# Two chunks' decay steps out of the first order, a block's plan turned by two units, and some low parts by TensorE, in a fused recurrence and feed-forward kernel

## The chip, the cores and the metric

One core of a Trainium2 chip. The metric is the device time of one execution in microseconds; of the kernel before three runs are shown, with a median of 519.06 us (518.17 to 519.08).

## The reference

A linear recurrence over 768 steps for 4 sequences and 8 heads of 48 channels, and a two-layer feed-forward with the gate h cos(h) on its output, for 3072 rows:

```python
for t in range(S):
    cur = einsum('bhd,bhe->bhde', u * k[t], v[t])
    y[t] = einsum('bhd,bhde->bhe', r[t], state + cur)
    state = w[t][..., None] * state + einsum('bhd,bhe->bhde', k[t], v[t])
...
h = x @ w_in                 # 3072 x 384 by 384 x 2048
out = (h * cos(h)) @ w_out   # 2048 x 384
```

## The kernel before

**Work.** The sequences are cut into 24 chunks of 128 steps (numbers 0 to 23 in the order in which they are taken); two chunks make a block of 256 rows, so there are 12 blocks. For each chunk the recurrence is put into products over the chunk, with running products of the decays; for each block the feed-forward runs over 8 units of 256 hidden channels. Every product of the feed-forward is taken with operands split into a high and a low part (fp32r), three products for one: high by high, high by low, low by high. The 16 weight blocks are loaded in a packed form in the first stage, turned to high and low parts, and stay.

**Names in the orders.** A number behind a name is a chunk, a block, a unit or a weight block; `+n` in a plan counts from the block at work. For a chunk: ld/load its r, k and decays, lv/v its values, lr its r and k by rows; e the backward scan of decays (line 254), f a reciprocal and the forward scan (259, 260), W a copy of the whole products; k and r the products of k and r with them (269, 271, 273); q and pc, cd (chunks under 6) or m, u, c (later ones) the diagonal; A the diagonal put into a tile by GpSimd (306); a the scores on TensorE (345, 353), P their masked copy by VectorE (363, 366); t and K a transpose and its copy; d, pp the state's decay. For a block: o, p the outputs of the recurrence (429 to 448), s the new states (397), n their sum; xh and xl (X) the high and low part of x. For a unit: mm1 (line 519, in the first order m0.t and m1.t, its two halves), the gate's steps I (ScalarE, 483), S (VectorE, 486), N (ScalarE's sine, 499), M (VectorE, 500), H (high part, ScalarE), L (low part, GpSimd, line 168), and mm2 (538). For a weight block: raw the load, wl and wg two unpackings by ScalarE (185, 189), wy their sum by VectorE (197), wc the high part by ScalarE (193), wx the low part by VectorE (199). Helpers at lines 165 and 168 hold all copies and subtractions.

**Order.** Each engine works through its own instructions in order, and the order is written by hand. `START` is the first order, one list for all five engines: everything of blocks 0 and 1 and of the weights, with the first decay steps of later chunks among it. Its units run in the sequence that `PAIR` gives (a 0 is block 0, a 1 is block 1). `Dn` issues n fillers (line 649): products of the identity by itself, in fp32, two instructions each, into a bank that the next mm1 overwrites. From block 2 on the eight rows of `PLAN` say what goes with each unit of a block; mm2 follows mm1 by two units. `FIRST` replaces the first rows for block 2 (six rows before), `LAST` those at the end. In the last units the decays are also checked (`check_decays`, from `slots - CHECK` on).

**Buffers that the argument touches.** mm1 writes one of two banks ("h" in `BANKS`, in the steady blocks), which the M of two units earlier frees. `maskf` is made by GpSimd, and its 8-bit copy `mask` by VectorE at line 707, ahead of `START`.

Of the kernel before, what the change touches and what calls it, by code (L numbers as in the profile page):

```python
# [70 lines left out]
m0.4 I3 wg8 q5 M2 e5 pc5 wc6 H2 L1 S3 m1.4 m0.5 v4 I4 wy9 N3 S4 cd4 mm2.1 wx6 wg7 wc9 M3 m1.5 wx9 N4 H3 L2 M4 wl7 I5  # L71
wl8 wy7 mm2.2 L3 m0.6 mm2.3 S5 wy8 wc7 wx7 H4 m1.6 raw13 N5 M5 wl11 raw10 e4 wg11 m0.7 wy11 L4 I6 mm2.4 raw12 wc8 S6
wx8 ld6 N6 M6 k5 W4 m1.7 H5 m0.8 k4 cd5 t5 t4 wc11 L5 I7 S7 H6 m1.8 L6 A4 d5 wg10 mm2.5 N7 K4 d4 A5 wl10 W5 I8 raw14
wx11 K5 pp5 M7 m0.9 mm2.6 wy10 S8 H7 N8 wc10 m1.9 f5 M8 wx10 wl12 f4 wl13 I9 m0.10 H8 wg13 S9 L7 N9 r4 mm2.7 a4 L8 e7
m1.10 M9 wg12 wy13 H9 L9 m0.11 wy12 I10 wc13 mm2.8 S10 wg14 m1.11 wx13 P4 raw15 wc12 N10 wx12 I11 M10 wl14 S11 H10 r5
N11 mm2.9 m0.12 s2 M11 wl15 wy14 n2 m1.12 wg15 H11 wy15 m0.13 a5 I12 L10 S12 L11 P5 wc14 wx14 m1.13 wc15 N12 mm2.10 I13
e6 M12 H12 mm2.11 m0.14 S13 wx15 o2 pp4 f6 N13 m1.14 M13 r6 H13 k7 W6 I14 L12 L13 m0.15 S14 p2 N14 xh2.0 k6 m1.15 xl2.0
I15 M14 S15 xh2.1 xl2.1 N15 mm2.12 M15 mm2.13 H14 H15 L14 L15
# [824 lines left out]
```

## Time and profile before

| | us |
|---|---|
| median of three runs (lowest, highest) | 519.06 (518.17, 519.08) |
| the profiled execution, its own time | 517.84 |
| its span, first to last instruction | 516.0 |
| TensorE busy | 508.4 |
| VectorE busy | 390.2 |
| ScalarE busy | 260.2 |
| GpSimd busy | 209.8 |

The span is what the profile shows of one execution; its own time has 1.84 us more around it. A busy time is the union of an engine's instructions, whether they are of use or not. PE stands for TensorE, DVE for VectorE, ACT for ScalarE, POOL for GpSimd, SP for SyncE, which issues the transfers; PEld are TensorE's weight loads, which run beside its products.

### The profile page before, as it was taken

To read this page: it belongs to the slowest core of one execution; us is meant where nothing else is said; L and a number is where in the kernel's file an instruction comes from. 1 tells how busy PE (TensorE), PEld (TensorE's weight loads), DVE (VectorE), ACT (ScalarE), POOL (GpSimd) and SP (SyncE) were. 2 spreads that over 40 slices of the span, in tenths; PEclk is the share of its full clock that TensorE was granted. 3 is DMA by queue.
4 is the path that set the end of the run, shared out by engine and by line. 5 is a ranking of instruction groups with operands and counts; after the bars stand their busy time and mean duration, and the time that the engine had idled before them with its cause. 6 is when DMAs were issued, how large, how long until landed. Compare 5 with 4: busy or idle time off the path is not lost.

```text
span 516.0 us, 12941 instructions
## 1 busy us (share of the span) xinstructions
PE 508.4 (99%) x5432; PEld 494.0 (96%) x5432; DVE 390.2 (76%) x662; ACT 260.2 (50%) x442; POOL 209.8 (41%) x275
## 2 busy tenths in 40 slices
PE   7999999999999999999999999999999999999997
PEld 7999999999999999999999999999999999999996
DVE  8897999977888768758858857947956957678333
ACT  1577997755444444444444444444344454444543
POOL 3361487344435334344334334343533533423330
PEclk9999999999999999999999999999999999999999
DMA  8998083063240151061061060160150130050001
GB/s 246 373 300 268 13 317 109 6 173 120 81 126 32 41 166 32 32 174 32 33 174 33 32 176 6 57 163 15 62 159 25 62 124 1 32 184 1 32 0 36
DMA packets 16733, 52.24 MB, mean 101 GB/s; under 512 B 2016, under 2 KB 8416, under 8 KB 16672
## 3 DMA queue, kind: packets, MB, share of 16 engines
q1 hardware_dynamic: 16528, 51.28, 32.3%
q8 instruction: 44, 0.72, 0.6%
q14 instruction: 17, 0.14, 0.1%
q10 hardware_dynamic: 144, 0.10, 0.1%
HBM read 46.65 MB, written 4.72 MB: 100 GB/s over the span
## 4 chain that ended last, share of the span: by engine, by line
PE 91%; DVE 4%; ACT 2%; DMA 1%; issue 1%; SPq 0%
PE ph L519 38%; PE acc L538 36%; PE filled L649 3%; PE pa L353 3%; PE py L429 2%; PE pst L397 2%; PE py L434 2%; PE pt L375 1%; PE pa L345 1%; PE py L448 1%; DVE h L197 1%; DMA u_by_head<-ut 1%; PE py L444 1%; DVE w L199 1%; PE pc L282 1%
## 5 line engine op out<-in xcount | busy, mean ns | idle before, releaser
L168 POOL TENSOR_TENSOR gs<-rr,gs 128x256 fp32r<-128x256 f32 x188 | 153.8, 838 | 240.7 <-ACT gs L165 235.9
L519 PE MATMUL ph<-xT,w 128*128 128x256 f32 x1728 | 222.4, 282 | 0.3
L519 PEld LDWEIGHTS ph<-xT,w 128*128 128x128 f32 x1728 | 213.0, 188 | 3.2 <-issue 0.6
L538 PE MATMUL acc<-w,gs 128*128 128x384 f32 x1152 | 215.2, 337 | 0.0
L538 PEld LDWEIGHTS acc<-w,gs 128*128 128x128 f32 x1152 | 196.1, 188 | 0.0
L499 ACT ACTIVATE rr<-rr,quarter 128x512 f32<-128x512 f32 x96 | 69.5, 724 | 96.6 <-DVE rr L486 96.5
L486 DVE SCALAR_TENSOR_TENSOR rr<-rr,ph 128x512 f32<-128x512 int32 x96 | 65.5, 682 | 69.4 <-ACT rr L483 68.9
L165 ACT CAST gs<-rr 128x512 fp32r<-128x512 f32 x96 | 59.5, 620 | 68.7 <-DVE rr L500 47.9
L500 DVE TENSOR_TENSOR rr<-rr,ph 128x512 f32<-128x512 f32 x96 | 65.5, 682 | 24.8 <-ACT rr L499 22.3
L483 ACT ACTIVATE rr<-ph 128x512 int32<-128x512 f32 x96 | 57.3, 597 | 48.9 <-PE ph L519 48.3
L306 POOL TENSOR_SCALAR_AFFINE_SELECT asb<-cd 128x512 f32<-128x512 f32 x48 | 41.6, 891 | 42.2 <-DVE cd L296 27.2
L366 DVE COPY_PREDICATED asb<-turned_mask,pa 64x128 f32<-64x128 uint8 (+1 forms) x108 | 33.6, 346 | 1.7
L260 DVE TENSOR_TENSOR_SCAN tt<-tt,inj 112x516 f32<-112x516 f32 x24 | 32.0, 1334 | 0.8
L254 DVE TENSOR_TENSOR_SCAN ee<-tt,one_e 112x516 f32<-112x516 f32 x24 | 31.9, 1328 | 0.1
L649 PE MATMUL filled<-ident 128*128 128x128 f32 x180 | 23.5, 289 | 1.9 <-POOL ident masks.py:199 1.9
L649 PEld LDWEIGHTS filled<-ident 128*128 128x128 f32 x180 | 22.3, 203 | 2.1 <-POOL ident masks.py:199 1.9
L185 ACT ACTIVATE h<-raw 128x768 int32<-128x768 uint32 x16 | 14.6, 916 | 13.0 <-DMA raw<-wts 11.9
L168 DVE TENSOR_TENSOR xT<-py,xT 128x384 fp32r<-128x384 f32 x24 | 12.3, 550 | 11.2 <-ACT xT L165 11.2
L165 ACT COPY past<-dd 48x192 f32<-48x192 f32 x40 | 14.0, 351 | 11.3 <-DVE dd L329 11.0
L197 DVE CUSTOM_DVE_ANT_0 h<-h,top 128x1536 uint16<-128x1536 uint16 x16 | 17.0, 1071 | 3.2 <-ACT cd L165 1.8
L189 ACT ACTIVATE top<-raw 128x768 f16<-128x768 bf16 x16 | 17.3, 1079 | 0.0
L199 DVE TENSOR_TENSOR w<-h,w 128x768 fp32r<-128x768 f32 x16 | 15.6, 973 | 0.3 <-ACT w L193 0.3
(77 smaller groups left out, 363.2 us busy)
## 6 DMA issues: line engine op xcount, KB each, us to landing
tt<-tr SPq DMA_DIRECT2D x22, 674.2 KB, 7.3
raw<-wts SPq DMA_DIRECT2D x16, 767.8 KB, 9.4
rk<-tn SPq DMA_DIRECT2D x18, 384.0 KB, 3.0
v<-tv SPq DMA_DIRECT2D x24, 224.0 KB, 5.5
ww<-w SPq DMA_DIRECT2D x6, 768.0 KB, 5.6
out<-ob SPq DMA_DIRECT2D x23, 192.0 KB, 2.0
tt<-tr SPq DMA_DIRECT2D x4, 224.0 KB, 4.6
tt<-tr SPq DMA_DIRECT2D x2, 226.2 KB, 3.8
```

Of the source, the lines that this page charges most:

```text
L165: (nc.scalar.copy if E[name] is nc.scalar else E[name].tensor_copy)(out=out, in_=in_)
L168: E[name].tensor_tensor(out=out, in0=full, in1=high.bitcast(F32), op=ALU.subtract)
L260: nc.vector.tensor_tensor_scan(out=wp[:, 0:W129], data0=wp[:, 0:W129], data1=inj.rearrange("p a t -> p (a t)"), initial=0.0, op0=ALU.mult, ...
L306: nc.gpsimd.affine_select(out=asb, in_=col.unsqueeze(2).to_broadcast([C, NP, C]), pattern=[[0, 4], [1, C]], compare_op=ALU.is_equal, fill= ...
L366: nc.vector.copy_predicated(*(which(x) for x in (a["asb", h], turned_mask, pa[h])))
L483: nc.scalar.activation(made["rr"].bitcast(I32), ph, AF.Copy, scale=INV2PI / W_SCALE, bias=0.25)
L486: nc.vector.scalar_tensor_tensor(out=made["rr"], in0=made["rr"].bitcast(I32), scalar=-2.0 * math.pi * W_SCALE, in1=ph, op0=ALU.mult, op1=A ...
L499: N=lambda: nc.scalar.activation(made["rr"], made["rr"], AF.Sin, scale=1.0 / W_SCALE, bias=quarter),
L500: M=lambda: nc.vector.tensor_tensor(out=made["rr"], in0=made["rr"], in1=ph, op=ALU.mult), H=high, L=low)
L519: nc.tensor.matmul(out=ph[:, fi], lhsT=wgt[u * FU + fi][:, 0, a, kt * 128:(kt + 1) * 128], rhs=xT[:, b, kt], start=n == 0, stop=n == 3 * K ...
L538: nc.tensor.matmul(out=accs[i][j][:, :DM], lhsT=gs[:, a, fi, j * C:(j + 1) * C], rhs=wgt[u * FU + fi][:, 1, b], start=u == 0 and fi == 0 a ...
L649: nc.tensor.matmul(out=filled, lhsT=ident, rhs=ident, start=True, stop=True)
```

## The change

- In `START`, e6, f6, W6, r6, k6, e7 and k7 are gone and the order is new; there are 33 fillers where there were 90. W0 becomes `Wa0`, the same copy by ScalarE.
- Weight blocks 0 and 2: wx is replaced by `wp` and `wv`. wp lets TensorE form identity times the whole value (fp32) plus minus-identity times the high part (fp32r) in a bank, for each of two halves; wv copies both to the low part by ScalarE. The same for x of block 0: `xp` adds minus-identity times the high part onto the bank that holds x, and `xa` copies it, in place of xl.
- The negative identity is new, made by ScalarE; it shares its place with `u_sb`, which is taken only when it is loaded.
- `mask` is copied by ScalarE.
- `PLAN`: the former rows 6 and 7 stand first, for the following block, with d of the odd chunk moved to row 3 and u, c, lr in row 1. `FIRST` has eight rows and takes the decay steps of chunks 6 and 7.
- The check of the decays begins 12 units before the end, not 14. `START` and the rest lie in one hand-written schedule, SyncE's part of it for `START` alone.

```diff
-PLAN = ["t+2 t+3 load+6 mm1 K+2 K+3 e+4 I S k+4 N M mm2 H L f+4",
-        "mm1 I S r+4 N M mm2 H L",
+PLAN = ["mm1 I S k+3 N M mm2 H L f+3",
+        "mm1 I S r+3 N M mm2 H L u+3 c+3 lr+5",
+        "t+2 t+3 load+6 mm1 K+2 K+3 e+4 I S k+4 N M mm2 H L f+4",
+        "mm1 I S r+4 N M mm2 H L d+3",
         "a+2 a+3 mm1 P+2 P+3 I S m+4 N M mm2 H L",
         "mm1 I S u+4 N M mm2 H L",
         "o+1 p+1 s+1 mm1 load+7 lv+6 lv+7 X+1 n+1 I S c+4 N M mm2 H L d+4",
-        "mm1 I S m+5 N M mm2 H L e+5 lr+6",
-        "mm1 I S k+5 N M mm2 H L f+5 d+5",
-        "mm1 I S r+5 N M mm2 H L u+5 c+5 lr+7"]
+        "mm1 I S m+5 N M mm2 H L e+5 lr+6"]
 START = """
-ld1 ld0 e1 f1 ld3 q1 raw1 e0 wl1 q0 k1 f0 D18 pc1 W0 q3 W1 r1 r0 wg1 ld2 D24 a1 k0 cd1 wy1 D2 t0 raw0 A1 v0 e2 pc0 P1
-q2 D7 a0 cd0 raw3 wl0 v1 t1 e3 wg0 raw2 K1 K0 raw4 raw5 wc1 wy0 A0 P0 wx1 raw6 wc0 D16 o0 wg2 ld7 k2 xh0.0 f2 pc2 wx0
-xh0.1 xl0.0 wg3 wl2 pc3 xl0.1 v3 cd2 t2 cd3 raw7 k3 wy2 D8 m0.0 f3 wc2 wl3 s0 wx2 wg4 K2 t3 m1.0 r2 wl4 v2 r3 I0 wy3 n0
-wy4 v5 A3 S0 wc3 K3 wg6 W2 A2 ld4 D3 m0.1 wc4 a2 raw9 D7 s1 a3 wx3 N0 wg5 m1.1 P2 n1 I1 P3 M0 H0 wx4 W3 wl5 wy5 D5 o1
-wl6 ld5 wc5 S1 wx5 xh1.0 xl1.0 xh1.1 L0 xl1.1 m0.2 wg9 mm2.0 N1 raw8 q4 M1 m1.2 m0.3 I2 pc4 wl9 S2 wy6 m1.3 raw11 H1 N2
...
+ld1 ld0 e1 raw0 f1 q1 e0 W1 Wa0 wl0 q0 D19 pc1 cd1 wg0 k1 k0 v0 raw1 ld3 A1 f0 r1 v1 D8 t0 pc0 t1 r0 wy0 a1 raw2 K0 K1
+ld2 cd0 wc0 wl1 P1 a0 raw3 wp0 A0 P0 wg1 raw4 v5 o0 e3 wv0 q3 wy1 f3 xh0.0 s0 xh0.1 pc3 wl2 k3 W3 q2 xp0.0 wg2 xp0.1 D3
+pc2 v3 wc1 xa0.0 wy2 e2 xa0.1 wc2 n0 wx1 cd3 cd2 r3 f2 W2 t3 m0.0 wg3 wp2 wl3 wy3 a3 raw5 m1.0 K3 v2 ld4 r2 wv2 A3 A2
+wc3 wl4 raw7 k2 I0 wg4 m0.1 wg5 wx3 P3 t2 a2 m1.1 raw6 wl5 raw8 P2 K2 v4 ld5 raw9 D3 o1 wy4 wy5 wc4 wc5 wx4 S0 s1 m0.2
+xh1.0 wx5 xl1.0 xh1.1 xl1.1 N0 I1 wg6 m1.2 M0 H0 m0.3 q4 I2 S1 L0 N1 S2 wl6 pc4 M1 m1.3 N2 I3 wy6 H1 S3 wc6 m0.4 N3 M2
...
+m0.9 t5 m1.9 k4 wx10 L6 A5 I9 N8 L7 r4 wl12 wx11 S9 wg12 K5 mm2.6 M8 mm2.7 a4 H8 N9 m0.10 wy12 A4 P4 M9 wl13 wg13 L8
+wc12 t4 wy13 m1.10 m0.11 H9 I10 pp5 mm2.8 S10 m1.11 N10 wc13 wg14 wx12 M10 I11 wx13 m0.12 L9 mm2.9 H10 wl14 f5 wg15 S11
...
 """
-FIRST = ["lr+2 lr+3 load+4 load+5 lv+4 lv+5 t+2 t+3 mm1 K+2 K+3 f+3 I S m+2 N M mm2 H L u+2 c+2 lr+4",
-         "mm1 I S r+3 N M mm2 H L m+3 u+3 c+3",
-         "mm1 I S N M mm2 H L d+2 d+3 lr+5 load+6 e+4",
...
+FIRST = ["lr+2 lr+3 load+4 load+5 lv+4 lv+5 mm1 e+2 e+3 k+2 k+3 I S f+2 N M mm2 H L r+2",
+         "mm1 I S f+3 N M mm2 H L r+3",
+         "mm1 t+2 t+3 I S K+2 K+3 N M mm2 H L m+2 u+2 c+2 d+2",
+         "mm1 I S m+3 u+3 N M mm2 H L c+3 d+3 lr+4",
+         "a+2 a+3 mm1 P+2 P+3 I S e+4 N M mm2 H L k+4",
+         "mm1 I S f+4 N M mm2 H L r+4 load+6",
+         "o+1 p+1 s+1 mm1 load+7 lv+6 lv+7 X+1 n+1 I S N M mm2 H L m+4 u+4 c+4 d+4",
+         "mm1 I S m+5 N M mm2 H L e+5 lr+6"]
-CHECK = 14
+CHECK = 12
@@
+    nident = cst.tile([C, KT, C], F32R, tag="u_sb", name="nident")[:, 0]
+    nc.scalar.activation(nident, ident, AF.Copy, scale=-1.0)
@@
+        def left_over():
+            made["left"] = [bank("a", [128, 512], "left")[:, :DM] for k in range(2)]
+            for k in range(2):
+                nc.tensor.matmul(out=made["left"][k], lhsT=ident, rhs=made["h"][:, k].bitcast(F32), start=True, stop=False, skip_group_check=True)
+                nc.tensor.matmul(out=made["left"][k], lhsT=nident, rhs=wgt[f][:, k, 0], start=False, stop=True, skip_group_check=True)
+
+        def taken():
+            for k in range(2):
+                nc.scalar.copy(out=wgt[f][:, k, 1], in_=made["left"][k])
+
+        part(("wp", f), left_over)
+        part(("wv", f), taken)
@@
+        def less(side):
+            nc.tensor.matmul(out=py[side].rearrange("p k t -> p (k t)"), lhsT=nident, rhs=halves_of["x"][:, 0, side], start=False, stop=True, skip_group_check=True)
+
+        def taken(side):
+            nc.scalar.copy(out=halves_of["x"][:, 1, side], in_=py[side].rearrange("p k t -> p (k t)"))
@@
-    with tc.manual_schedule(engines={ET.PE, ET.DVE, ET.Activation, ET.Pool, ET.SP}):
-        nc.vector.tensor_copy(out=mask, in_=maskf)
-        for token in START.split():
-            at_first(token)
-    engines(LATER)
     up1 = [NU * BLK, NU * BLK - LAG]
     with tc.manual_schedule(engines={ET.PE, ET.DVE, ET.Activation, ET.Pool}):
+        with tc.manual_schedule(engines={ET.SP}):
+            nc.scalar.copy(out=mask, in_=maskf)
+            for token in START.split():
+                at_first(token)
+        engines(LATER)
```

## Rows read from the trace of the kernel before

**Rows 1.** The page's parts 1 and 2: busy time of TensorE; slices.

```profile
PE 508.4 (99%) x5432; PEld 494.0 (96%) x5432; DVE 390.2 (76%) x662; ACT 260.2 (50%) x442; POOL 209.8 (41%) x275
...
PE   7999999999999999999999999999999999999997
...
DVE  8897999977888768758858857947956957678333
...
PEclk9999999999999999999999999999999999999999
```

**Rows 2.** The page's part 5: groups of instructions (busy, mean ns, idle before).

```profile
L486 DVE SCALAR_TENSOR_TENSOR rr<-rr,ph 128x512 f32<-128x512 int32 x96 | 65.5, 682 | 69.4 <-ACT rr L483 68.9
...
L260 DVE TENSOR_TENSOR_SCAN tt<-tt,inj 112x516 f32<-112x516 f32 x24 | 32.0, 1334 | 0.8
L254 DVE TENSOR_TENSOR_SCAN ee<-tt,one_e 112x516 f32<-112x516 f32 x24 | 31.9, 1328 | 0.1
L649 PE MATMUL filled<-ident 128*128 128x128 f32 x180 | 23.5, 289 | 1.9 <-POOL ident masks.py:199 1.9
...
L168 DVE TENSOR_TENSOR xT<-py,xT 128x384 fp32r<-128x384 f32 x24 | 12.3, 550 | 11.2 <-ACT xT L165 11.2
...
L197 DVE CUSTOM_DVE_ANT_0 h<-h,top 128x1536 uint16<-128x1536 uint16 x16 | 17.0, 1071 | 3.2 <-ACT cd L165 1.8
...
L199 DVE TENSOR_TENSOR w<-h,w 128x768 fp32r<-128x768 f32 x16 | 15.6, 973 | 0.3 <-ACT w L193 0.3
```

**Rows 3.** Windows: length; PE, PEld, DVE, ACT, POOL busy; clock; DMA share, GB/s.

```profile
0.00:46.44 46.44, 43.15 (x520) 40.81 (x520) 39.61 (x54) 24.12 (x39) 18.34 (x26) 1.00 0.96 299
46.44:86.06 39.62, 38.83 (x293) 38.16 (x289) 38.35 (x47) 34.70 (x55) 23.34 (x25) 1.00 0.51 178
86.06:116.48 30.42, 30.42 (x334) 28.97 (x332) 26.11 (x40) 18.98 (x30) 13.10 (x14) 1.00 0.30 80
```

**Rows 4.** TensorE's timeline, 0 to 150 us (start, length, instructions, wait before).

```profile
1.87 5.75 PE L649 MATMUL filled<-ident 128*128 128x128 f32 x36 [1.87 <-POOL ident masks.py:199]
8.74 1.02 PE L282 MATMUL pc<-u_by_head,rkt 112*128 112x2 f32 x8 [1.12 <-DMA u_by_head<-ut]
9.63 5.60 PE L649 MATMUL filled<-ident 128*128 128x128 f32 x48
...
46.44 1.33 PE L519 MATMUL ph<-xT,w 128*128 128x256 f32 x9
47.61 2.24 PE L538 MATMUL acc<-w,gs 128*128 128x384 f32 x12
...
84.97 1.16 PE L345 MATMUL pa<-tt 48*128 48x128 f32 x16 [0.54 <-DVE tt L269]
```

**Rows 5.** VectorE's timeline, 0 to 145 us.

```profile
2.44 2.32 DVE L707 CAST mask<-maskf 128x512 uint8<-128x512 f32 x1 [0.37 <-POOL maskf L125]
4.68 1.21 DVE L254 TENSOR_TENSOR_SCAN ee<-tt,one_e 112x516 f32<-112x516 f32 x1
```

**Rows 6.** SyncE's timeline, 0 to 3.6 us: the first loads' issues.

```profile
0.83 2.75 SPq L225 DMA_DIRECT2D tt<-tr  x6
```

**Rows 7.** Transfers issued from 0.5 to 1.0 us: size, us to landing.

```profile
tt<-tr SPq DMA_DIRECT2D x1, 226.2 KB, 2.8
```

**Rows 8.** Groups by line of the whole run, those not on the page.

```profile
L165 ACT CAST xT<-py 128x384 fp32r<-128x384 f32 x24 | 10.5, 482 | 4.5 <-PE py L448 2.7 <-PE py L429 1.5 <-PE py L434 0.2
...
L271 DVE TENSOR_TENSOR tt<-tt,ee 112x256 f32<-112x256 f32 x18 | 10.0, 553 | 0.0
...
L363 DVE COPY_PREDICATED asb<-mask,pa 128x512 f32<-128x512 uint8 x12 | 8.1, 727 | 3.2 <-PE pa L345 3.2
...
L259 DVE RECIPROCAL inj<-ee 112x4 f32<-112x4 f32 x24 | 4.1, 172 | 0.0
```

**Rows 9.** Windows of block 2 and block 3, columns as in rows 3.

```profile
116.50:156.60 40.10, 40.10 (x457) 39.08 (x456) 32.65 (x62) 19.08 (x36) 18.70 (x25) 1.00 0.36 103
156.60:196.80 40.20, 40.20 (x458) 39.12 (x457) 29.98 (x56) 18.52 (x34) 16.24 (x23) 1.00 0.27 77
```

More of the change, by code (lines that the diff above doesn't have):

```diff
@@ L70 @@
-wl6 ld5 wc5 S1 wx5 xh1.0 xl1.0 xh1.1 L0 xl1.1 m0.2 wg9 mm2.0 N1 raw8 q4 M1 m1.2 m0.3 I2 pc4 wl9 S2 wy6 m1.3 raw11 H1 N2
[L71 to L78, printed above, removed]
-"""
-FIRST = ["lr+2 lr+3 load+4 load+5 lv+4 lv+5 t+2 t+3 mm1 K+2 K+3 f+3 I S m+2 N M mm2 H L u+2 c+2 lr+4",
[5 rows of a table removed]
+ld1 ld0 e1 raw0 f1 q1 e0 W1 Wa0 wl0 q0 D19 pc1 cd1 wg0 k1 k0 v0 raw1 ld3 A1 f0 r1 v1 D8 t0 pc0 t1 r0 wy0 a1 raw2 K0 K1
@@ new lines @@
+m1.6 M4 H4 d4 wy8 raw12 M5 raw11 raw10 wl9 I6 wg9 mm2.3 S6 m0.7 L4 N6 wc8 wy9 wc9 pc5 m1.7 mm2.4 cd5 wg10 f4 k5 H5 W4
+I7 M6 n1 wx8 H6 wl10 d5 m0.8 wx9 S7 L5 N7 wg11 wl11 M7 wy10 wy11 mm2.5 raw14 raw13 raw15 m1.8 I8 S8 wc10 wc11 ld7 H7
+m0.9 t5 m1.9 k4 wx10 L6 A5 I9 N8 L7 r4 wl12 wx11 S9 wg12 K5 mm2.6 M8 mm2.7 a4 H8 N9 m0.10 wy12 A4 P4 M9 wl13 wg13 L8
+wc12 t4 wy13 m1.10 m0.11 H9 I10 pp5 mm2.8 S10 m1.11 N10 wc13 wg14 wx12 M10 I11 wx13 m0.12 L9 mm2.9 H10 wl14 f5 wg15 S11
+m1.12 N11 L10 wl15 r5 I12 mm2.10 M11 wy14 m0.13 wc14 K4 S12 a5 wy15 W5 N12 wx14 H11 wc15 M12 m1.13 m0.14 P5 wx15 I13
@@ L86 @@
+H12 L11 S13 mm2.11 N13 pp4 m1.14 I14 M13 H13 m0.15 o2 m1.15 S14 I15 S15 L13 L12 N14 N15 p2 mm2.12 M14 xh2.0 xl2.0 M15
+mm2.13 H15 L15 xh2.1 s2 H14 xl2.1 ld6 n2 L14
+"""
+FIRST = ["lr+2 lr+3 load+4 load+5 lv+4 lv+5 mm1 e+2 e+3 k+2 k+3 I S f+2 N M mm2 H L r+2",
[7 rows of a table added]
 LAST = "mm1 I S N M", "mm1 I S N M mm2 h l", "mm2 h l"
-CHECK = 14
+CHECK = 12
 PAIR = "0001110101010101"
@@ L134, in rwkv_cos_ffn @@
     halves = cst.tile([R96, 2], F32, name="halves")
-    u_sb = cst.tile([C, DM], F32, name="u_sb")
     u_by_head = cst.tile([R, NP, 2], F32, name="u_by_head")
@@ L230, in att_load @@
         if j == BY_PE:
-            E["qt"].dma_start(out=u_sb, in_=u.to_broadcast([C, DM]))
+            told["u"] = cst.tile([C, DM], F32, tag="u_sb", name="u_sb")
+            E["qt"].dma_start(out=told["u"], in_=u.to_broadcast([C, DM]))
     def att_load_rk(a):
@@ L291, in att_diag @@
             part(("m", a["j"]), lambda: E["rk"].tensor_tensor(out=rk, in0=rk, in1=a["rk"][:, 1], op=ALU.mult))
-            part(("u", a["j"]), lambda: E["ru"].tensor_tensor(out=rk, in0=rk, in1=u_sb, op=ALU.mult))
+            part(("u", a["j"]), lambda: E["ru"].tensor_tensor(out=rk, in0=rk, in1=told["u"], op=ALU.mult))
             def sums():
@@ L464, in att_past @@
             part(("xl", (i, side)), lambda side=side: low(side))
+            if i <= BLK:
+                part(("xp", (i, side)), lambda side=side: less(side))
+                part(("xa", (i, side)), lambda side=side: taken(side))
     def att_x(a):
@@ L637, in at_first @@
     def at_first(token):
+        by = re.match(r"(W|H|wc)([av])(\d+)$", token)
+        if by:
+            name = dict(W="whole", H="gh", wc="whi0")[by[1]]
+            usual, E[name] = E[name], dict(a=nc.scalar, v=nc.vector)[by[2]]
+            parts.pop((by[1], int(by[3])))()
+            E[name] = usual
+            return
+        if token[:2] == "wp":
+            parts.pop(("wx", int(token[2:])))
+        if token[:2] == "wx":
+            for x in "wp", "wv":
+                parts.pop((x, int(token[2:])))
+        if token[:2] == "xp":
+            parts.pop(("xl", (int(token[2]), int(token[4]))))
+        if token[:2] == "xl":
+            for x in "xp", "xa":
+                parts.pop((x, (int(token[2]), int(token[4]))))
         n, at, side = re.match(r"(mm2\.|m[01]\.|[a-zA-Z]+)(\d+)(?:\.(\d))?$", token).groups()
```

1 line of the change is left out of this document (added), and 3 rows, old and new, of the table FIRST.

## The prediction

> **What bounds the kernel now.** I read the page's busy times first: TensorE is busy 508.4 of 516.0 us, and in the 40 slices it shows a gap in the first alone, while VectorE stands at 9 tenths in a run of slices near the start [rows 1]. So outside its first stage the kernel can become shorter only by doing less on TensorE. Among the groups of instructions one is no work at all: 180 instructions of line 649, the fillers, which multiply the identity by itself and whose result nobody reads [rows 2]. All 90 of them stand in the first order. By the windows, that stage ends at 116.48 us; in its first part, up to the first half of block 0's third unit (m0.2, at 46.44), TensorE is busy 43.15 us although all the fillers lie there, and VectorE 39.61; from there to 86.06 TensorE has 38.83 of 39.62, VectorE 38.35, ScalarE 34.70; after that both have room [rows 3]. The start is thus bound by the inputs of TensorE's work, with fillers in the waits; the middle is full on three engines; the rest is TensorE alone. A wait that shows this is in TensorE's timeline: at 84.97 the scores of chunk 4 stood 0.54 us for VectorE's product on line 269 [rows 4].
>
> **What the change does, part by part.** *Fillers.* The first order before has D18 24 2 7 16 8 3 7 5, which is 90; the new one D19 8 3 3, which is 33. Those taken out lie in the stretch that ran at 48 instructions in 5.60 us, two to a filler, so 0.233 us each [rows 4]. 57 x 0.233 = 13.3 us off TensorE's queue.
>
> *Low parts by TensorE.* wp0 and wp2 replace two subtractions of VectorE. Each is two products of 384 columns in full fp32 and two in fp32r. No fp32 product of 384 columns is in the trace. From above: at the fillers' pace per column it is 3 x 0.233 = 0.70 us; the fp32r one is 0.19 (12 of line 538 in 2.24, [rows 4]); so 2 x (0.70 + 0.19) = 1.78 each, 3.6 for both. From below: if all ran at line 538's pace, 4 x 0.19 x 2 = 1.5. I take the upper end, since the filler is the same form of product. The two xp add 2 x 0.19 = 0.4. Together 4.0, from below 1.9. Each adds a wait: wp0 for ScalarE's wc0, with o0 queued behind it, wp2 for wc2, with a3 and m1.0 behind. o0 waits for P0 in any case, which VectorE's list has behind wy0, the source of wc0; and wx1, for m1.0, stands behind wy2. So both are covered, as long as ScalarE keeps up.
>
> TensorE's sum to the end of the stage is then -13.3 + 4.0 = -9.3 us, all else being the same instructions: the two lists hold the same products. That holds if the inputs come as much earlier. At m0.2 it asks for 46.44 - 9.3 = 37.1 us.
>
> *VectorE ahead of m0.2.* I compared the two lists' VectorE entries before m0.2: 45 before, 35 after, and none that is new. Gone from there are the low parts of weights 0, 2 and 5 (3 x 0.97), four of x (4 x 0.55), one S and one M (2 x 0.68), and n1, which is ScalarE's [rows 2]. The mask's copy, 2.32 us, goes to ScalarE [rows 5]. Sum 2.9 + 2.2 + 1.4 + 2.3 = 8.8. If VectorE's waits stay as they are, m0.2 comes at 46.44 - 8.8 = 37.6, within 0.5 us of TensorE's sum. The mask's part counts only as far as data are there: the first load, issued at 0.83, lands 2.8 us later, at 3.6 [rows 6, 7], and the first scan began at 4.68 [rows 5]; so 1.0 of the 2.3 is sure at that point and the rest is gained only where VectorE would otherwise be last. The first weight block now follows directly on the loads of chunks 0 and 1, which lets ScalarE begin earlier on weights and adds no transfer. ScalarE gets a mask copy, the negative identity and six copies of low parts at 0.48 [rows 8]; it was busy 24.12 of 46.44 there [rows 3], so only the two copies ahead of m0.0 lie on the path, in place of two subtractions of 0.55 [rows 2]: nothing.
>
> *From m0.2 to m1.10.* Here VectorE had 1.27 us of slack. The new list holds between the two 1 more S, 2 M, 2 wy, 1 wx, 2 xl and 1 P, and 1 e and 1 f fewer: 3 x 0.68 + 2 x 1.07 + 0.97 + 2 x 0.55 + 2 x 0.73 - 1.33 - (1.33 + 0.17) = +4.9 us [rows 2, 8]. 38.35 + 4.9 = 43.2 against 39.6 of TensorE: 3.6 too much, if all of it had to be done by then. The last four of these (wy12, P4, M9, wy13) are for later units; they are 2 x 1.07 + 2 x 0.73 + 0.68 = 4.3, and without them 38.9 fits. So the cost lies between 0 and 3.6. I take 1.5: the balance is even on average, but the single deadlines (block 1's first unit needs M0 and two xl, the units after it the subtractions of weights 6 to 8) come in bunches. ScalarE too has more listed there than before and had 4.9 us of slack [rows 3]; I add nothing for it.
>
> *Chunks 6 and 7 out of the first order.* e6 f6 r6 k6 e7 k7 are VectorE's: 2 x 1.33 + 1.50 + 3 x (2 x 0.55) = 7.5 us [rows 2, 8]. Before, all but e7 lay behind m1.10, where VectorE had room, 26.11 of 30.42 [rows 3]: taking them out gains nothing. They go to the first turned block, 116.5 to 156.6 before, where VectorE was busy 32.65 of 40.10 [rows 9]: it becomes 40.2 of 40.1, full. What could stop TensorE there: two units in, mm1 needs the bank that M of the first unit frees. Ahead of that M the queue holds e6 e7 k6 k7 S f6 M, 2.7 + 2.2 + 0.7 + 1.5 + 0.7 = 7.8 us, against two units of 2 x (2.1 + 2.1) = 8.4 (mm2 is 2.24 with its tail, [rows 4]). It fits with 0.6 to spare; later deadlines have more. e6 also waits for ld6, now last in SyncE's list, but behind nothing that waits longer than for a weight block's place, and the last block is unpacked well before the stage ends. Cost 0, at worst 1.5 if the queue comes late out of the first stage.
>
> *The block turned by two units.* The same steps, each two units later against the block's own use, d of the odd chunk five. The steady block has TensorE busy 40.20 of 40.20 and VectorE 29.98 [rows 9]. The tightest new distance: o, p, s stand in unit 6, and the next block's first mm1 follows two units on, so 8.4 us for two copies of 0.48, two subtractions of 0.55 and the queue ahead. Cost 0; what covers it are those two units, and if they were not enough it would cost up to a unit part in each of nine blocks, which I hold for excluded by VectorE's 10 us of slack per block. The loads issued in unit 2 and 6 instead of 0 and 4 keep their distance to their scans, since those move too. The w checks move by two units into the same idle end, cost 0.
>
> Sum: -13.3 + 4.0 + 1.5 = -7.8 us. Against the profiled execution's own 517.84 us that is 510.0; that run lies 1.2 below the median of 519.06, so the median becomes **511.2 us**. Ends: -13.3 + 1.9 = -11.4 gives 507.7; -13.3 + 4.0 + 3.6 + 1.5 = -4.2 gives 514.9.
>
> **The rivals.** *First, VectorE holds the middle and the turned block.* For it: 97% busy from 46.44 to 86.06 and the 0.54 us wait [rows 3, 4]. Against it: what is needed by m1.10 just fits. Both upper ends together and the 0.5 us of m0.2 give -4.2 + 0.5 = -3.7: 515.4 us. Chance 0.16.
>
> *Second, the fillers only stood in waits, and the waits stay.* Then the removed 13.3 us return as idle time, and the time is the old one, 519.1, or up to 1 above for products that now come late. For it: every filler is in the stage in which TensorE waits for others. Against it: VectorE's queue ahead of m0.2 really is 8.8 us shorter, and VectorE was the busy one there with 39.61 of 46.44 [rows 3]. Chance 0.05.
>
> *Third, on the other side: without fillers TensorE drops to its lower clock.* At the start the fillers took 5.75 / 36 = 0.160 us an instruction on the mean, later 0.117, with the granted clock shown as 1.00 (the upper level, 2.4 GHz); a wait of 1.12 us before 8.74 was followed by the quick pace [rows 1, 4]. So a slow pace exists, and a short wait did not bring it. If the products from 9.6 us to m0.2, 27 us of them, ran at that slow mean, they would take 27 x 0.160 / 0.117 = 37 us: 10 more, 521 us; at the lower level, 1.2 GHz, throughout, twice as long, 538. I take 521. The Trainium skill (TensorE: Matmul & The Clock Gate, Part 1) says that TensorE begins at half its clock and falls back to it when it stands idle; by that rule removing fillers is a risk. The trace agrees on the slow beginning, and no run here shows a fall. The mechanism decides when one wait is much longer than those 1.12 us, such as one for a late weight block; walking the new list with the durations above I find none over 1. Chance 0.06.
>
> **How the numbers follow.** Forecast 0.73, the rivals 0.16, 0.05, 0.06. The forecast and the first rival are faster by over 0.2% (1.0 us, which is about what a measurement of this kernel can tell from no change): 0.89. Same 0.05, slower 0.06. The range takes in both ends and the first rival: 507.7 to 515.6.
>
> **What would show it.** Right: line 649 with 66 instructions; m0.2 near 37 to 39 us; the first mm1 of block 2 near 109; the turned block at 40.1 to 40.6 with VectorE above 38; later blocks at 40.2. Wrong: waits of TensorE that sum to over 4 us between 10 and 38 us (second rival, and, with slow products, the third), a wait for VectorE before m0.6 to m0.10 or at the second and third unit of block 2 (first rival), or a steady block longer than 40.2 us, which would upset the turned plan.

## The result, and the profile after

The changed kernel takes **511.24 us** (median of 4 runs, 509.65 to 512.88) against 518.62 (518.16 to 519.08) for the kernel before in the same job: a ratio of 0.9858, 95% interval 0.9824 to 0.9892. It is faster by 7.4 us, where 511.2 us had been forecast. The profiled execution took 512.88 us, the longest of the four, with a span of 511.0. Line numbers are now the changed kernel's: fillers 692, first product 545, second 564, low parts of weights 208 and 209.

The page's busy times and slices, which answer to [rows 1]:

```profile
PE 502.7 (98%) x5332; PEld 487.5 (95%) x5332; DVE 377.4 (74%) x657; ACT 263.5 (52%) x451; POOL 200.4 (39%) x274
...
PE   8899999999999999999999999999999999999997
...
DVE  6799999658779858947947956966965975677633
...
PEclk9979999999999999999999999999999999999999
```

New is the third digit of PEclk (the clock that TensorE was granted, in tenths of full speed), a 7: it was lower for a part of the slice from 25.6 to 38.3 us. The windows (columns as in [rows 3]) are cut at the first product of block 0's third unit (m0.2, now at 42.49), 39.62 us behind it as in [rows 3], at the first product of block 2, and one block further each:

```profile
0.00:42.49 42.49, 37.71 (x421) 34.42 (x421) 35.46 (x49) 24.90 (x45) 12.42 (x23) 0.92 0.97 290
42.49:82.11 39.62, 39.57 (x297) 38.93 (x296) 36.86 (x49) 36.16 (x56) 23.33 (x26) 1.00 0.69 218
82.11:111.43 29.32, 29.32 (x328) 27.91 (x326) 18.21 (x26) 19.94 (x34) 9.45 (x14) 1.00 0.25 70
111.45:151.55 40.10, 40.10 (x457) 39.08 (x457) 32.97 (x67) 18.11 (x34) 17.98 (x25) 1.00 0.38 104
151.55:191.75 40.20, 40.20 (x458) 39.14 (x458) 31.29 (x58) 18.60 (x34) 16.91 (x23) 1.00 0.28 85
```

Block 2 begins at 111.43 in place of 116.48, 5.05 us earlier, and the span is 5.0 shorter. So all of the gain lies in the first order, and what follows takes as long as before (399.6 us against 399.5). Inside the first order m0.2 comes 3.95 earlier and the rest is 1.1 shorter (68.94 against 70.04): TensorE has no wait left there. But m0.2 had been expected at 37 to 39. TensorE's timeline shows what holds it (start, length, wait before):

```profile
16.12 0.91 PE L208 MATMUL left<-h,ident 128*128 128x384 f32 x2
16.58 0.64 PE L209 MATMUL left<-w,nident 128*128 128x384 f32 x1
17.05 0.81 PE L208 MATMUL left<-h,ident 128*128 128x384 f32 x2
17.40 0.63 PE L209 MATMUL left<-w,nident 128*128 128x384 f32 x1
17.97 0.68 PE L446 MATMUL py<-asb,v 128*32 128x128 f32 x14
...
21.06 0.94 PE L299 MATMUL pc<-u_by_head,rkt 112*128 112x2 f32 x7
24.29 0.16 PE L299 MATMUL pc<-u_by_head,rkt 112*128 112x2 f32 x1 [2.29 <-issue]
...
26.16 1.87 PE L299 MATMUL pc<-u_by_head,rkt 112*128 112x2 f32 x8
...
28.56 2.27 PE L545 MATMUL ph<-xT,w 128*128 128x256 f32 x9
```

A stop of 2.29 us stands in the middle of eight like products, between the seventh and the eighth, so it is no wait for data; the profile says "issue". After it the clock goes down, by the windows of 2 us:

```profile
22.00:24.00 2.00, 0.00 (x1) 0.03 (x1) 0.94 (x2) 1.65 (x2) 0.00 (x0) 1.00 0.96 255
24.00:26.00 2.00, 1.71 (x9) 1.71 (x8) 0.58 (x1) 1.66 (x4) 0.00 (x0) 0.64 0.99 381
26.00:28.00 2.00, 2.00 (x11) 1.91 (x11) 2.00 (x3) 0.99 (x3) 0.00 (x0) 0.50 1.06 407
28.00:30.00 2.00, 2.00 (x12) 2.00 (x12) 2.00 (x3) 2.00 (x6) 1.82 (x3) 0.50 1.06 413
30.00:32.00 2.00, 2.00 (x8) 1.56 (x8) 2.00 (x2) 0.52 (x2) 1.36 (x3) 0.65 1.08 241
```

0.50 is the lower level, 1.2 GHz. The shortfall of the four windows from 24 on is 2 x (0.36 + 0.50 + 0.50 + 0.35) = 3.4 us. One transfer fits the stop: a packet on queue q8, "instruction", in flight from 21.59 to 22.87. The transfers of the microsecond in which it starts:

```profile
q1 hardware_dynamic: 51, 0.25, 100.5%
q8 instruction: 1, 0.02, 8.0%
```

By then TensorE had begun 444 instructions (products, weight loads and the few semaphore instructions among them counted), at the stop 449, and it went on 1.42 us after the packet had ended. The packets of q8 keep step with TensorE: there are 43 of them for its 10,810 instructions, one for every 251. So it looks as if TensorE ran out of instructions while the queues were full. VectorE, too, waited in its timeline for chunk 2's load, as it did not in the old order:

```profile
25.42 0.69 DVE L262 TENSOR_TENSOR rkt<-tt 112x512 f32<-112x512 f32 x1 [2.48 <-DMA tt<-tr]
```

That product ended at 26.11, and the pc that needs it began at 26.16. From 25.42 to m0.2 VectorE was busy 16.68 of 17.07 us.

Three theories went into the runs: **fetch and clock** (the stop and the lower level after it set m0.2), **transfers** (the late load and VectorE's queue set it) and TensorE's own work.

### The profile page after: what moved, and what is told of

It is laid out like the page before. It is cut to its first block, busy times and chain, and to the rows that moved or that the text cites. A ratio compares the mean times of both kernels' runs of the same rounds, so it can differ in the third digit from the quotient of the medians.

```text
span 511.0 us, 12726 instructions
## 1 busy us (share of the span) xinstructions
PE 502.7 (98%) x5332; PEld 487.5 (95%) x5332; DVE 377.4 (74%) x657; ACT 263.5 (52%) x451; POOL 200.4 (39%) x274
## 4 chain that ended last, share of the span: by engine, by line
PE 96%; DVE 1%; DMA 1%; issue 1%; SPq 0%; ACT 0%; DVEq 0%
PE ph L545 40%; PE acc L564 39%; PE pa L370 3%; PE py L446 2%; PE py L451 2%; PE pst L414 2%; PE pt L392 2%; PE pa L362 1%; PE pc L299 1%; PE py L465 1%; DMA u_by_head<-ut 1%; PE py L461 1%; PE filled L692 1%; PE left L208 1%; SPq L241 0%
## 5 line engine op out<-in xcount | busy, mean ns | idle before, releaser
L171 POOL TENSOR_TENSOR gs<-rr,gs 128x256 fp32r<-128x256 f32 x188 | 147.9, 808 | 241.9 <-ACT gs L168 241.4
L526 DVE TENSOR_TENSOR rr<-rr,ph 128x512 f32<-128x512 f32 x96 | 65.6, 683 | 24.3 <-ACT rr L525 21.9
L323 POOL TENSOR_SCALAR_AFFINE_SELECT asb<-cd 128x512 f32<-128x512 f32 x48 | 38.2, 821 | 43.3 <-DVE cd L313 35.5
L277 DVE TENSOR_TENSOR_SCAN tt<-tt,inj 112x516 f32<-112x516 f32 x24 | 29.6, 1234 | 0.8
L168 ACT CAST xT<-py 128x384 fp32r<-128x384 f32 x24 | 10.5, 481 | 11.5 <-PE py L465 10.8
L200 DVE CUSTOM_DVE_ANT_0 h<-h,top 128x1536 uint16<-128x1536 uint16 x16 | 15.9, 1004 | 0.4 <-ACT top L192 0.3
L446 PE MATMUL py<-asb,v 128*32 128x128 f32 x384 | 15.5, 276 | 0.0
L196 ACT CAST w<-h 128x768 fp32r<-128x768 f32 x16 | 13.2, 830 | 4.1 <-DVE h L200 4.1
```

The source lines that it names most:

```text
L168: (nc.scalar.copy if E[name] is nc.scalar else E[name].tensor_copy)(out=out, in_=in_)
L171: E[name].tensor_tensor(out=out, in0=full, in1=high.bitcast(F32), op=ALU.subtract)
L277: nc.vector.tensor_tensor_scan(out=wp[:, 0:W129], data0=wp[:, 0:W129], data1=inj.rearrange("p a t -> p (a t)"), initial=0.0, op0=ALU.mult, ...
L323: nc.gpsimd.affine_select(out=asb, in_=col.unsqueeze(2).to_broadcast([C, NP, C]), pattern=[[0, 4], [1, C]], compare_op=ALU.is_equal, fill= ...
L526: M=lambda: nc.vector.tensor_tensor(out=made["rr"], in0=made["rr"], in1=ph, op=ALU.mult), H=high, L=low)
```

## The experiments

Each edit is against the changed kernel, unless it says otherwise; most are of the list START. The kernel before took 518.3 to 518.5 us (medians) in all four jobs.

**1. The changed kernel again.** 

> The changed kernel once more, beside the next three on one chip. Both theories: 509.5 to 513 us, and a wait of TensorE near 22 us followed by some us at half the granted clock, of a length that differs from run to run.

511.58 us (5 runs, 510.1 to 513.06), ratio 0.9873 (0.9854 to 0.9892). The stop is there again, 1.74 us, m0.2 at 41.34. Its time moves by 3 us from run to run, that of the kernel before by 1.4 in this job (16 runs), but by 3.5 in a later one (11 runs, 517.76 to 521.21). It goes with the mean clock: of the nine executions of this list here and in the result, the two at 0.997 or more took 509.65 and 510.1 us, the seven at 0.993 or less 511.58 (median).

**2. Chunk 2's load ahead of weight block 2.**

```diff
-raw1 ld3 A1 f0 r1 v1 D8 t0 pc0 t1 r0 wy0 a1 raw2 K0 K1 ld2 cd0
+raw1 ld3 A1 f0 r1 v1 ld2 D8 t0 pc0 t1 r0 wy0 a1 raw2 K0 K1 cd0
...
-pc3 wl2 k3 W3 q2 xp0.0 wg2 xp0.1 D3 pc2 v3 wc1 xa0.0 wy2 e2 xa0.1 wc2 n0 wx1
+pc3 k3 W3 q2 xp0.0 xp0.1 D3 pc2 v3 wc1 xa0.0 e2 xa0.1 wl2 wg2 wx1 wy2 wc2 n0
```

> Chunk 2's load is issued ahead of weight block 2's, and the two unpackings of that block by ScalarE stand behind the two copies of x's low part. Theory 'transfers' (VectorE's wait of 2.48 us for chunk 2's load, ending at 25.4, sets when m0.2 comes, 42.5): the load lands some 3 us earlier, that wait falls under 0.5 us, m0.2 comes at 40 to 41, and the time is 1.5 to 2.5 us under that of the changed kernel. Theory 'clock' (the 6.7 us that TensorE runs at half its clock from 24.5 on cost their 3 us in full): the wait of 2.3 us at 22 that brings it on is no wait for data and stays, so the time stays within 0.7 us of the changed kernel's.

511.12 us (6 runs, 508.63 to 513.58), 0.9857 (0.983 to 0.9885): no difference. VectorE made chunk 2's q product at 22.00, 3.4 us earlier, and the pc that waits for it came at 26.18 all the same, since the stop lay in between. By VectorE's timeline its wait moved to weight block 2. ScalarE unpacked that block late, from 25.56 on; it had waited 3.81 us for TensorE's xp, which came behind the stop, and for no load:

```profile
22.00 0.69 DVE L262 TENSOR_TENSOR rkt<-tt 112x512 f32<-112x512 f32 x1
...
27.45 0.96 DVE L200 CUSTOM_DVE_ANT_0 h<-h,top 128x1536 uint16<-128x1536 uint16 x1 [2.77 <-ACT top L192]
```

TensorE's timeline of the same run:

```profile
24.09 0.16 PE L299 MATMUL pc<-u_by_head,rkt 112*128 112x2 f32 x1 [2.59 <-issue]
```

The load alone does not set m0.2, which came at 43.17.

**3. Chunk 2's decay later.** q2, e2, f2 and pc2 behind m1.0; wc1, wx1 and the low parts of x ahead of weight block 2.

> The loads stay; in VectorE's order the steps on chunk 2 (q2, e2, f2) go behind wx1 and r3, on TensorE pc2 goes behind m1.0, and on ScalarE wc1 and x's low parts go ahead of weight block 2. Theory 'transfers': what waited for chunk 2's load and weight block 2 no longer stands in front of m0.0; m0.0 comes at 24 to 26 instead of 28.6, but VectorE's later queue keeps much of it: m0.2 at 40.5 to 41.5, the time 1 to 2 us under that of the changed kernel. Theory 'clock': as long as TensorE stops at 22 us for 2.3 us, the half clock follows, and the time stays within 0.7 us.

515.11 us (11 runs, 511.36 to 520.33), ratio 0.994 (0.9912 to 0.9969) without the two longest. The median of the other nine is 514.82, 3.2 us slower than run 1: a miss for both theories. The trace is of the longest, 520.33: there the stop stayed (2.6 us), and a second wait, of 2.3 us, ended at 40.65, for VectorE's masked copies, with a second fall of the clock. What made the shorter ones slower than run 1 is not shown. Several steps moved at once, so the run says only that this order is worse.

**4. Low parts by VectorE again.** wp and xp dropped, wv and xa turned into wx and xl.

> The low parts of weight blocks 0 and 2 and of block 0's x go back to VectorE, everything else as in the changed kernel. By the prediction's sum TensorE has 4.0 us less and VectorE 2 x 0.97 + 2 x 0.55 = 3.0 us more ahead of m0.2. Theory 'transfers': three of the four fall into VectorE's wait for chunk 2's load, the subtraction of weight block 2 stands behind it, so 0.5 to 1.5 us more than the changed kernel. Theory 'VectorE's own queue is the bound throughout': all 3.0 us more. Theory 'clock': TensorE has 2.5 us less work in and before the slow stretch, so 1 to 2 us less than the changed kernel.

512.5 us (6 runs), 0.9914 (0.9891 to 0.9938): 0.9 more than run 1, the intervals just touching. The instruction packet came at 18.86, with 344 instructions begun, and there was no stop; but TensorE waited 1.8 us for chunk 2's q product and 1.5, 1.0 and 0.9 us for VectorE at other places, and the clock fell as well. So it falls after waits for data too. Of the theories, 'transfers' had named this size (0.5 to 1.5 more); 'clock' had asked for 1 to 2 us less and missed. Moving the low parts to TensorE is worth some 1 us by the medians, 2 by the ratios, hardly clear of the noise.

**5. Twelve fillers ahead of the stop.**

```diff
-o0 e3 wv0 q3 wy1 f3 xh0.0 s0 xh0.1 pc3
+o0 e3 wv0 q3 wy1 f3 D12 xh0.0 s0 xh0.1 pc3
```

> The changed kernel with 12 fillers (12 x 0.233 = 2.8 us of TensorE) put between the two runs of short products at 17.97 to 21.06 us, so that TensorE has fewer instructions begun when its first instruction fetch lands. Theory 'fetch and clock' (TensorE runs out of instructions at the 450th, stands 1.7 to 2.6 us, and then works at the lower clock level for some 6.7 us): the stop before the second pc goes under 0.7 us, the granted clock stays at 1.00 from 24 to 32 us, the mean clock is 0.998 or more, and the time falls to 509.0 us (508.3 to 510.0), against 511.4 of the changed kernel. Theory 'transfers' (chunk 2's load and VectorE's queue set the second pc at 26.2 and all behind it): the clock may stay up, but the first product of unit 0 comes at 28 to 29 us as before and the time stays at 511.4, within 0.7. Theory 'TensorE's own work' (fillers cost what they take): 514.2.

511.45 us (4 runs), 0.9858 (0.9841 to 0.9875). The stop went down to 0.78 us, and three executions of four kept a clock of 0.999 or more; but those took 510.3 to 512.0, not 509, and the profiled one (0.992) 513.9. That is a miss for 'fetch and clock': 2.9 us of fillers bought back about what they cost. The first product of unit 0 came at 29.01, and 'transfers' had named that place and this time.

**6. The same twelve behind the stop.**

```diff
-q2 xp0.0 wg2 xp0.1 D3
+q2 xp0.0 wg2 xp0.1 D15
```

> The same 12 fillers, but added to the three that already stand behind the stop, ahead of the second pc. Theory 'fetch and clock': they can't fill a stop that lies before them, so the stop of 1.7 to 2.6 us and the lower level stay, and the fillers themselves run at half speed and push the second pc back: 513 to 516 us, mean clock 0.988 to 0.993. Theory 'fillers of any place keep the clock': 509 to 510, as the run with fillers in front. Theory 'transfers': 511.4 to 513, since the second pc waits for data until 26.2 in any case.

513.05 us (5 runs), 0.9898 (0.9879 to 0.9916); the stop 1.76 us. The place counts, as 'fetch and clock' had it: 1.6 us more than with the fillers in front. But the forecast clock did not come (0.993 to 1.000 in place of 0.988 to 0.993), and two executions at 1.000 took 511.64 and 513.05, so it is not the clock alone that makes this difference.

**7. The turned plan with the old first order** (START from the kernel before; the plan, the first block, the checks and the mask by ScalarE from the changed one).

> The changed kernel with the old list of the first order: so the turned plan, the new first block, the checks two units later and the mask by ScalarE alone, with all 90 fillers and the low parts by VectorE. The prediction's step (each of these costs nothing): 518.4 us as before, within 0.7 (ratio 0.9987 to 1.0013). The first rival (VectorE holds the turned block): 521 to 523. If the gain came from the plan and not from the list: 511 to 514.

518.4 us (10 runs), 1.0002 (0.9993 to 1.0011). These parts cost nothing and bring nothing.

**8. The kernel before with 33 fillers.**

```diff
-D18 ... D24 ... D2 ... D7 ... D16 ... D8 ... D3 ... D7 ... D5
+D18 ... D4 ... D2 ... D3 ... D3 ... D1 ... D1 ... D1
```

> The kernel before with 33 fillers in place of 90, each group cut to about a third, and nothing else changed. The prediction's first term taken by itself (a filler is 0.233 us of the path): 57 x 0.233 = 13.3 us less, 505.1 us. The second rival (the fillers of the old order only stand in waits for loads and for VectorE): the time stays at 518.4, within 1, and waits of some 10 us in all appear at TensorE before 46 us. The third rival (without the fillers the clock falls too): 519 to 523, with the granted clock at 0.5 in part of the first 46 us.

518.88 us (10 runs, 514.52 to 521.47), 0.9998 (0.9973 to 1.0022): 57 fillers less, and no gain. In the trace (of the longest execution, 521.47) stand in place of them waits, by the table of TensorE's waits (in total, times, longest), and stretches at the lower level, from 12.0 to 25.6 and from 39.3 to 49.5 us (0.977 over the run), by windows:

```profile
PE pst L397 <- DMA v<-tv: 3.3, 1, 3.3
PE pa L345 <- DVE tt L269: 3.2, 2, 2.7
```

```profile
18.00:20.00 2.00, 1.74 (x6) 1.22 (x6) 2.00 (x3) 0.49 (x2) 2.00 (x3) 0.50 1.02 403
...
42.00:44.00 2.00, 2.00 (x24) 1.91 (x24) 0.00 (x0) 0.54 (x2) 0.00 (x0) 0.50 1.06 243
```

The waits are 6.5 us. In the two stretches TensorE was busy 20.7 of 23.9 us, so the lower level cost it some 10 us (an estimate, half of that). The two executions with the highest mean clock, 0.990, are the shortest, 514.52 and 516.77.

**9. s0 behind, wide fillers.** The 32 short products of s0 go behind the third group of fillers, and that group becomes 4 fillers of 512 columns, each of which takes 0.90 us for four instructions (two products, two weight loads).

```diff
-f3 xh0.0 s0 xh0.1 pc3 wl2 k3 W3 q2 xp0.0 wg2 xp0.1 D3
+f3 xh0.0 xh0.1 pc3 wl2 k3 W3 q2 xp0.0 wg2 xp0.1 V4 s0
...
+        elif n == "V":
+            tags = BANKS[stage[0]]["h"]
+            filled = ps.tile([C, 4, C], F32, tag=tags[(turn["h"] + 1) % len(tags)], name="filled")
+            for again in range(j):
+                nc.tensor.matmul(out=filled, lhsT=ident, rhs=ident.unsqueeze(1).to_broadcast([C, 4, C]), start=True, stop=True)
```

> The changed kernel with the 32 short products of s0 (1.13 us) moved behind the third group of fillers, and that group made of 4 fillers four times as wide in place of 3 narrow ones, so that TensorE begins 64 instructions fewer ahead of its first instruction fetch and has some 3.7 us of work of few instructions meanwhile; no engine but TensorE changes. Theory 'fetch and clock': no stop over 0.8 us between 17 and 28 us, granted clock 1.00 from 24 to 32 us, mean clock 0.998 or more in most executions, second pc (chunk 2) still near 26.2 because its data come then, and 509.2 us (508.5 to 510.2), with a spread under 2 us. Theory 'transfers': the clock holds but the first product of unit 0 and all behind it stay where they were, 511.4 within 0.7. Theory 'TensorE's own work': 0.93 x 4 - 0.7 = 3.0 us more, 514.4.

510.51 us (6 runs, 509.07 to 511.66), 0.9839 (0.9813 to 0.9866). The stop is gone and the mean clock is 0.998 or more in all six executions; TensorE's timeline, and windows of it:

```profile
20.99 3.60 PE L697 MATMUL filled<-ident 128*128 128x512 f32 x8
24.51 1.13 PE L414 MATMUL pst<-v,kn 128*64 128x48 f32 x32
25.57 1.05 PE L299 MATMUL pc<-u_by_head,rkt 112*128 112x2 f32 x8
...
39.80 2.39 PE L545 MATMUL ph<-xT,w 128*128 128x256 f32 x18
```

```profile
24.00:26.00 2.00, 2.00 (x38) 1.43 (x36) 2.00 (x4) 1.07 (x3) 0.00 (x0) 1.00 1.00 406
26.00:28.00 2.00, 2.00 (x20) 2.00 (x20) 2.00 (x3) 1.58 (x6) 1.90 (x3) 1.00 1.06 406
```

In the profiled executions m0.2 moves from 42.49 (in run 1, 41.34) to 39.80 although TensorE does 2.9 us more. That the stop goes when fewer instructions are begun, and that the clock then holds, is shown. That the two set the time is not: 0.7 us came against the result and 1.1 against run 1, less than the 2 expected, with overlapping intervals. In this run the fillers stand in the wait for chunk 2's q product, which ends at 24.0. From there VectorE works without a wait (busy 2.00, 2.00, 1.97, 2.00, 2.00 and 2.00 in the windows from 24 to 36 us) to the masked copies that block 1's first output product, o1, needs. They end at 36.62, and o1 begins at 36.85. VectorE's timeline:

```profile
23.34 0.69 DVE L262 TENSOR_TENSOR rkt<-tt 112x512 f32<-112x512 f32 x1 [1.12 <-DMA tt<-tr]
...
34.02 2.60 DVE L380 COPY_PREDICATED asb<-mask,pa 128x512 f32<-128x512 uint8 x4
```

**10. Both early.** Run 2's list with s0 behind m0.0, two wide fillers, and r3, f2, wx1 and m1.0 ahead of the work on weight block 2.

> The kernel with chunk 2's load issued ahead of weight block 2 (the second run), and s0 behind the first product of unit 0, two wide fillers in place of the three narrow ones, chunk 3's r product, chunk 2's f and wx of block 1 ahead of the work on weight block 2 on their engines, and m1.0 ahead of the products of wp2. If the stop for instructions hid the gain of the early load in the second run: the second pc starts at 23 to 24 us, the first product of unit 0 at 25 to 26.5, that of unit 2 at 38.5 to 40.5, and the time is 507.5 us (506 to 509). If something else sets unit 2 (weight block 2 or VectorE's queue): the start moves but the product of unit 2 stays at 41 to 43 and the time at 509 to 511.5.

515.22 us (6 runs), 0.993 (0.9903 to 0.9957): a miss. m0.0 came at 23.22, 5.3 us earlier than in the changed kernel, and then TensorE and VectorE both waited for ScalarE, and the clock stood at 0.50 from 34 to 44 us (timelines of TensorE, VectorE and ScalarE):

```profile
32.45 0.91 PE L208 MATMUL left<-h,ident 128*128 128x384 f32 x2 [2.06 <-ACT kn L168]
```

```profile
32.06 0.96 DVE L200 CUSTOM_DVE_ANT_0 h<-h,top 128x1536 uint16<-128x1536 uint16 x1 [3.03 <-ACT h L188]
```

```profile
29.07 0.83 ACT L196 CAST w<-h 128x768 fp32r<-128x768 f32 x1 [4.01 <-DVE h L200]
```

TensorE waits for the copy K3, VectorE for weight block 3. Both stood on ScalarE behind weight block 2's high part, which waited 4.01 us for VectorE's sum of that block; in the new list that sum came only behind wx1, r3 (3.01 us) and f2. No engine waited for a load there: the order of the list moved the wait, not the transfers.

**11. Fillers in the middle.** Run 9 with 4 wide fillers ahead of the first product of unit 7.

```diff
-mm2.3 S6 m0.7 L4
+mm2.3 S6 V4 m0.7 L4
```

> The run with s0 behind, and 4 wide fillers (some 3.7 us of TensorE) ahead of the first product of unit 7, in the middle of the first order, near 75 us. If TensorE bounds the middle (it showed no wait there after the change): 3.7 us more than the run with s0 behind, block 2 starting that much later. The prediction's step (VectorE and ScalarE bound the middle, +1.5 us over TensorE's work): 0 to 2 us more, since fillers would take the place of waits.

514.27 us (6 runs), 0.9923 (0.9896 to 0.995): 3.76 us more than run 9, the whole of the fillers' 3.60. In run 9 that product starts at 60.12, here, by TensorE's timeline, at 64.09:

```profile
60.44 3.60 PE L697 MATMUL filled<-ident 128*128 128x512 f32 x8
64.09 1.33 PE L545 MATMUL ph<-xT,w 128*128 128x256 f32 x9
```

TensorE bounds the middle.

**12. Run 9 trimmed.** V3 for V4, D2 for the last D3, r3 ahead of wx1.

> The run with s0 behind, trimmed where its trace showed slack: 3 wide fillers in place of 4 (chunk 2's q product ended at 24.0 us while TensorE came to it at 25.6), chunk 3's r product ahead of wx of block 1 on VectorE (the bank of the fourth pa waited for it 0.2 us and stood idle before that), 2 fillers for 3 ahead of o1. If TensorE has room there: unit 0's product at 26.0 in place of 26.8, that of unit 2 at 38.8 to 39.4 in place of 39.8, clock 0.999 or more, 509.7 us (508.8 to 510.5). If VectorE's queue (the copies under the mask that end at 36.6 us) sets unit 2: nothing, 510.5 within 0.6. If the fillers taken out let the clock fall: 511 to 512.

510.48 us (5 runs, 510.11 to 511.07), 0.9841 (0.9823 to 0.986): nothing gained, as forecast for the case that VectorE's queue sets unit 2. m0.2 came at 40.28. On VectorE a scan that took 1.23 us before ran 3.35 us, beside work of GpSimd, and the product for chunk 2's k came late; the transpose behind it started 0.1 us after that product's end, though the profile calls the wait "issue" (VectorE's timeline, then TensorE's):

```profile
28.52 3.35 DVE L277 TENSOR_TENSOR_SCAN tt<-tt,inj 112x516 f32<-112x516 f32 x1
...
33.23 0.68 DVE L286 TENSOR_TENSOR tt<-tt,ee 112x512 f32<-112x512 f32 x1
```

```profile
34.02 0.57 PE L392 MATMUL pt<-ident,tt 112*128 112x112 f32 x4 [1.45 <-issue]
```

Side by side, from the traces (us; "begun" counts TensorE's products, weight loads and semaphore instructions; the q product is chunk 2's, by VectorE):

| run | first instruction packet | begun by then | stop | q product | start of m0.2 | span less that |
|---|---|---|---|---|---|---|
| before | 17.74 | 250 | none | 19.57 | 46.44 | 469.6 |
| changed | 21.59 | 444 | 2.29 | 25.42 | 42.49 | 468.5 |
| 1 | 20.67 | 438 | 1.74 | 23.02 | 41.34 | 468.6 |
| 2 | 21.62 | 449 | 2.59 | 22.00 | 43.17 | 468.5 |
| 4 | 18.86 | 344 | none | 23.21 | 40.93 | 468.6 |
| 5 | 21.26 | 396 | 0.78 | 22.79 | 43.66 | 468.5 |
| 6 | 20.43 | 436 | 1.76 | 23.91 | 42.17 | 468.5 |
| 9 | 20.89 | 391 | none | 23.34 | 39.80 | 468.7 |
| 12 | 21.21 | 393 | none of this kind | 24.23 | 40.28 | 468.9 |

The last column says where the time is decided: behind m0.2 each of these takes the same. And in all six traces with a stop (run 3 too) it stands ahead of the same instruction by number, TensorE's 450th, be it a pc product or, in run 5, the middle of s0; it ended 1.26 to 1.47 us after the packet. A wait for data or for a bank to write to would not count instructions: it is TensorE's supply of them.

Neither theory sets m0.2 alone. Without a stop and at full clock (9, 12) it comes 16.1 to 16.5 us behind the q product, with VectorE busy all the time. In the changed kernel's trace it comes 17.1 behind, so the late load explains most of its lateness, and the stop and the clock some 0.6 us. In run 1, with the load 2.4 us earlier, it comes 18.3 behind: there they cost some 1.9 us. These are estimates from the differences.

## Why the prediction was right, and where its steps failed

The total was right to 0.1 us, by errors that cancelled.

- **Fillers and low parts: right as a sum of TensorE's work.** It asked for m0.2 at 37.1. Measured are 42.49, less the stop of 2.29 and the 3.4 us that the lower level took, 36.8; from run 9, 39.80 less 2.9 of added fillers, 36.9. As a time it was not to be had: run 12, with one wide filler less than run 9, began m0.2 no earlier. One wp takes 17.97 - 16.12 = 1.85 us against 1.78, so the upper end was the one to take. But 57 fillers are worth 13.3 us only together with the new list: in the old one they were worth nothing (run 8). That is the second rival's time, but by the third rival's means as much: 6.5 us of waits and some 10 at the lower level in its trace.
- **"Walking the new list I find none over 1": the step that failed.** It let m0.2 come when the work of the engines was done. There was a stop of 2.29 us for instructions, which no queue of the list shows, and VectorE waited 2.48 us for a load that the prediction had priced at nothing ("adds no transfer"). Thus neither TensorE's 37.1 nor VectorE's 37.6 came about: +5.4 us. Of the stop, not all was paid: the second pc, at 26.16, had to wait for VectorE's product until 26.11 in any case.
- **VectorE ahead of m0.2: 8.8 forecast, mis-sized.** The count goes by the list. In the old run S1, wx5 and the two xl of block 1 (0.68 + 0.97 + 2 x 0.55 = 2.75 us) stand ahead of m0.2 in the list but ran behind its start at 46.44, by VectorE's timeline before:

```profile
47.12 0.67 DVE L486 SCALAR_TENSOR_TENSOR rr<-rr,ph 128x512 f32<-128x512 int32 x1
48.09 0.96 DVE L199 TENSOR_TENSOR w<-h,w 128x768 fp32r<-128x768 f32 x1 [0.30 <-ACT w L193]
48.97 1.02 DVE L168 TENSOR_TENSOR xT<-py,xT 128x384 fp32r<-128x384 f32 x2
```

  They had not held it, so the same sum, with the mask's 2.3 in full, gives 46.44 - 6.05 = 40.4. Runs 9 and 12, without a stop, have 39.80 and 40.28.
- **The third rival came in part**, at the place where it said it would decide (a wait longer than 1.12 us): 3.4 us of TensorE's pace lost at the lower level in the profiled execution; the two groups of executions in run 1 lie 1.7 us apart. The Trainium skill (TensorE: Matmul & The Clock Gate, Part 1) has the fall after idle time; the traces here now show it, in stretches at 0.50. The length of a wait does not decide alone: behind the stop of 0.78 us in run 5 the clock fell (0.50 in the window from 28 to 30 us), through the wait of 1.45 us in run 12 it held (1.00 from 32 to 36).
- **The middle: +1.5 forecast, -1.1 measured.** VectorE and ScalarE were not the bound: TensorE was busy 39.57 of 39.62, the 0.79 us of waits in [rows 3] are gone, and added products cost their full time (run 11). VectorE was busy 36.08 us up to m1.10 (81.33), where 38.9 to 43.2 had been counted; the sum added S1, wx5 and two xl to a window that already held them. The first rival falls with it.
- **The turned plan and chunks 6 and 7: 0 forecast, 0 measured** (run 7, and 399.6 against 399.5 us behind the first order). But VectorE is busy 32.97 of the turned block, not above 38: the prediction added chunks 6 and 7 to the old block's steps and did not take off those that the turn by two units moves out at its end, by [rows 9] some 30 x 2/8 = 7.5 us (an estimate).
- **The mask:** the first scan began at 3.64 in place of 4.68, the 1.0 us that was called sure.

For the profiled execution 510.0 was forecast and 512.88 came: +5.4 at m0.2, -2.6 in the middle, +0.1 behind. The median of the changed kernel lies 1.6 below its profiled execution, where 1.2 above had been added; that closed the gap, by the luck of which execution was profiled: it is the longest of the four. The range would have held for any of them.

## What to carry to other kernels

Sum the work of the engine that bounds, but then ask of the new order what is not in any list: does the bounding engine get its instructions in time, and where does it stand still and lose its clock? Count by the trace, not by the list, what an engine had done when a stage ended. Fillers that stand in waits are worth nothing to remove until the inputs come earlier, and they can be what holds the clock up; where a stage's end and the start of the next are a constant apart, one timestamp (here m0.2) judges every variant. A load brought forward gains only if no other step of the hand-written order then waits in its place.
